# Attention and FFN in one kernel: 78 steps of the hand-kept plan are given to the engines at another tick

## The chip, the cores and the metric

One core of a Trainium2 chip runs the whole program in one launch. The metric is device time in microseconds of that core. The kernel before takes 844.36 us, the median of 3 runs (844.21 to 844.95).

## The reference

Attention over 8 sequences of 576 positions with 8 heads of 64; heads 0 to 3 see a window of the last 32 positions, heads 4 to 7 every fourth of the last 128. Its output, seen as 4608 tokens of 512 numbers, goes through a feed-forward layer of width 2048 with an exact GELU.

```python
scores = scale * np.matmul(q, k.transpose(0, 1, 3, 2))
scores = np.where(masks[None, :, :, :], scores, -1000000000.0)
attn = np.exp(scores - np.max(scores, axis=-1, keepdims=True))
attn = attn / (np.sum(attn, axis=-1, keepdims=True) + 1e-09)
x = np.matmul(attn, v)          # 8 x 8 x 576 x 64, then to 4608 x 512
h = x @ w_in                    # 4608 x 2048
g = 0.5 * h * (1.0 + erf(h / sqrt(2)))
out = g @ w_out                 # 4608 x 512
```

## The kernel before, in words

The tokens are cut into nine chunks of 512: the first 512 positions of each sequence (chunks 0 to 7), and the eight remainders of 64 together (chunk 8). Attention works on a pair of heads at a time ("5.2" is chunk 5, head pair 2): scores on TensorE (L307), softmax in place on ScalarE (`softmax`, L428, one activation with a running sum per 64 keys), the division and a transpose on VectorE (`norm_half`, `turn_both`), four exchanges of rows by DMA (`swap_keys`, L383), the weighted sum on TensorE (`av_four`, L573; `av_last`, L530, for chunk 8) and the way back to SBUF (`x_back` on VectorE, L586; `x_wide` on ScalarE, L594).

Every number of the feed-forward layer is held as a high part and a residual ("low") in fp32r, and a product of two blocks is three matmuls for each of two halves of 128 rows: high by high, residual by high, high by residual.

Chunks 0 to 2 go through the feed-forward layer plainly (L605, L628). From chunk 3 on the kernel takes two chunks and two blocks of the weights as a 2 by 2 block product and forms it from seven products, M1 to M7, in place of eight (L1044). There are three pairs of chunks, (3, 4), (5, 6) and (8, 7), and four groups of weights. One pair with one group is called a **round** here: 14 products for the first layer (the **H half**: M1 to M7 for two output blocks, called e0 and e1), then 14 for the second (the **O half**: M1, M5, M6, M2, M7, M3, M4, each for e0 and e1). A product is six matmuls of 128 x 512. R1 to R12 are the rounds in order of time; R1 begins 326.0 us after the span's start.

In a H half ScalarE copies M1 from its bank to another one (L1069) before M6 may be added in the first, stashes M6 and M5 (L1065), and applies GELU; VectorE adds (L1073, L1076). The results are the four block values B11, B12, B21, B22 and the combinations T1 = B12 - B11 (L1092), T3 = B22 - B12 (L1093), T2 = B22 - T1 (L1094), T4 = B21 - T2 (L1095). Of seven of these ScalarE rounds the high part (L1090) and VectorE subtracts the residual (L1091): the operands of the O half, B11 for M1, T1 for M5, T2 for M6, B21 for M2, T3 for M7, B22 for M3, T4 for M4.

In an O half sums of products are formed in PSUM: ScalarE copies M1 out of banks 2 and 3 (L1101, "first copy"), M6 is added there, ScalarE copies the sum again to banks 0 and 1 (L1101, "second copy") as soon as these are emptied of M5, then M7 is added, then M4. Four accumulators in SBUF, C11, C12, C21 and C22, and M5 take the banks over: by ScalarE in the first round of a pair (L1107), by VectorE in the others (L1109). C22 must be taken out of banks 2 and 3 before M4 may start there, C21 before the next round's M1 is copied into them.

The operands of the next pair of chunks (`combine`: high part L923, residual L928, combinations L936) are made the same way, beside the last round of the pair before. The weights of the seven products come from DRAM into a ring of five tiles (`ring_load`, L997), one tile for the two products that share it, on SyncE's queue, which also carries the loads of q, k and v, the exchanges, and the finished outputs (L1129).

The order of the work is written by hand. The products stand in a fixed order. All other work from chunk 2's attention on is a list of 1237 **steps**; `add(at, rank, gen)` gives a step a tick (one product is one tick; R1 begins at tick 96 and each round is 28 ticks) and a rank. The list is sorted by tick, rank and place in the list (L1183), and after each product the steps whose tick has come are given to the engines (`upto`, L758). Each engine takes its instructions strictly in that order, so a tick sets only which instruction stands ahead of which on an engine; it sets no time.

Of the kernel before, what the change touches and what calls it, by code (L numbers as in the profile page):

```python
# [46 lines left out]
TICKS = 28  # L47
ORDER = (2, 3, 0, 1)
SLOTS = 5

SUBTRACT = ()
SCHEDULE = """
# [35 lines left out]
def attn_ffn(ctx: ExitStack, tc: tile.TileContext, qk, qk_lp, qk_ld, v, v_ld, w, outT):  # L88
# [662 lines left out]
    steps = []  # L751

    def add(at, rank, gen):
        steps.append((at, rank, len(steps), gen))

    at = 0

# [57 lines left out]
    def prepare(u, at, dt):  # L815
        s = {}
        add(at, 5, unit_whole(s, u))
        for i in range(4):
            add(at + (3 + .5 * i) * dt, 5, unit_sums(s, u, i))
        for n in range(2):  # L820
            add(at + (4 + n) * dt, 6, unit_high(s, u, n))
            add(at + (4.5 + n) * dt, 6, unit_low(s, u, n))
            add(at + (6 + n) * dt, 6, keep_sums(s, u, n))
# [135 lines left out]
    def ring_tile(n):  # L959
        n %= SLOTS  # L960
        if n not in ring:
            ring[n] = xg.tile([P, 2, N], F32R, tag="xg", name="ring")
        return ring[n].rearrange("p a (b c) -> p (a b) c", b=2)
# [23 lines left out]
    def ring_load(n):  # L987
        yield "q"
        j, q, kind, m = tiles[n]
        to = ring_tile(n).bitcast(F32)  # L990
        off = DM if kind == "O" else 0
        if m in SUMS:
            src, off = sd[ORDER[q]][:, SUMS[m]], off // 2
        else:
            i, k = HELD[kind][m]
            src, off = wd[ORDER[q]][i], off + 2 * P * k
        nc.sync.dma_start(to, src.rearrange("p u (l c) -> p (u l) c", l=2)[:, :, off:off + 2 * P])  # L997
    for n in range(len(tiles)):
        add(P0 - 7.5 + .3 * n if n < SLOTS else P0 + last_use[n - SLOTS] + 2, 4, ring_load(n))

# [332 lines left out]
```

## Time and profile before

| | |
|---|---|
| median of 3 runs | 844.36 us |
| the profiled execution | 845.09 us, span 843.3 us |
| TensorE matmul busy | 816.3 us, 97% of the span |
| TensorE weight load busy | 661.5 us, 78% |
| VectorE, ScalarE busy | 562.7 us (67%), 503.7 us (60%) |
| mean granted TensorE clock | 0.996 of full speed |
| DMA | 212.31 MB, 252 GB/s |

A timeline row gives the start, the length and the instructions run together, and in brackets how long the engine sat idle ahead of them and which instruction ended that wait. A wait for "issue" is one for which the profile names no releaser. A matmul row's length ends with the last matmul's result; the next row's start tells when TensorE's array was free again, so lengths of stretches are taken from start to start.

### The profile page before, as it was taken

How to read it: one execution, taken by the hardware profiler on the slowest of the kernel's cores; microseconds unless marked ns; L12 is line 12 of the kernel's file. 1: busy time of each engine (PE TensorE's matmuls, PEld its weight loads, DVE VectorE, ACT ScalarE, POOL GpSimd, SP SyncE). 2: the span in 40 equal slices, each digit the busy share in tenths (PEclk: the TensorE clock that was granted, in tenths of full speed). 3: DMA queues.
4: the chain of work that ended last, by engine and by line, in shares of the span. 5: the costliest groups of instructions: out<-in, count | busy, mean ns of one | idle time of the engine just before them, and what ended most of it. 6: DMA issues, size and time to landing. Idle time of an engine off the chain costs nothing.

```text
span 843.3 us, 19925 instructions
## 1 busy us (share of the span) xinstructions
PE 816.3 (97%) x8396; PEld 661.5 (78%) x8396; DVE 562.7 (67%) x675; ACT 503.7 (60%) x1149; POOL 57.7 (7%) x80
## 2 busy tenths in 40 slices
PE   7899999999999999989999999999999999999997
PEld 5687888888888888868787777777787788888885
DVE  8888863347676797545757786734657886172847
ACT  7597833735747565676555674857766646453442
POOL 2000020222305220000000000000000000000000
PEclk9999999999999999999999999999999999999999
DMA  9997478945998869876767688856466677665664
GB/s 362 416 419 303 152 300 323 373 154 189 318 359 296 294 212 331 254 233 194 271 203 274 193 296 258 284 185 225 144 218 222 205 249 238 197 189 191 197 197 152
DMA packets 118296, 212.31 MB, mean 252 GB/s; under 512 B 6848, under 2 KB 92864, under 8 KB 110784
## 3 DMA queue, kind: packets, MB, share of 16 engines
q1 hardware_dynamic: 118064, 210.79, 72.2%
q8 instruction: 66, 1.08, 0.5%
q10 hardware_dynamic: 144, 0.26, 0.1%
q14 instruction: 22, 0.18, 0.1%
HBM read 161.21 MB, written 42.99 MB: 242 GB/s over the span
## 4 chain that ended last, share of the span: by engine, by line
PE 75%; ACT 11%; DVE 10%; issue 2%; DMA 1%; SPq 0%; DVEq 0%; ACTq 0%
PE ps L1044 37%; PE ps L628 16%; PE ps L605 16%; PE ps L307 3%; ACT g L1090 3%; ACT sm L428 2%; PE ps L573 2%; DVE g L1091 2%; ACT ps L1101 1%; ACT xn L594 1%; DVE g_value L1093 1%; DMA raw_qk<-qk 1%; ACT L428 1%; DVE acc L1094 1%; DVE g_value L1076 1%
## 5 line engine op out<-in xcount | busy, mean ns | idle before, releaser
L1044 PE MATMUL ps<-g,ring 128*128 128x512 f32 x1008 | 239.0, 394 | 10.5 <-issue 3.4
L1044 PE MATMUL ps<-xc,ring 128*128 128x512 f32 x1008 | 237.1, 393 | 2.7 <-ACT ps L1069 2.7
L1044 PEld LDWEIGHTS ps<-g,ring 128*128 128x128 f32 x1008 | 188.3, 189 | 58.3 <-DVE g L1091 6.1
L1044 PEld LDWEIGHTS ps<-xc,ring 128*128 128x128 f32 x1008 | 189.0, 189 | 43.5 <-ACT ps L1069 3.3
L1091 DVE TENSOR_TENSOR g<-g_value,g 128x1024 fp32r<-128x1024 f32 x73 | 89.1, 1222 | 106.9 <-ACT g L1090 106.9
L605 PE MATMUL ps<-x,weight 128*128 128x512 f32 x576 | 137.5, 392 | 0.9 <-DVE x L550 0.6
L628 PE MATMUL ps<-g,weight 128*128 128x512 f32 x576 | 135.6, 392 | 0.0
L605 PEld LDWEIGHTS ps<-x,weight 128*128 128x128 f32 x576 | 107.1, 188 | 24.4 <-DVE x L550 1.0
L628 PEld LDWEIGHTS ps<-g,weight 128*128 128x128 f32 x576 | 107.3, 188 | 22.7
L1090 ACT CAST g<-g_value 128x1024 fp32r<-128x1024 f32 x73 | 76.2, 1048 | 38.2 <-DVE g_value L1093 21.9
L428 ACT ACTIVATE sm<-sm,st 128x64 f32<-128x64 f32 (+1 forms) x224 | 75.6, 339 | 0.9 <-DVE st L359 0.7
L617 DVE TENSOR_TENSOR g<-gf,g 128x512 fp32r<-128x512 f32 x48 | 35.9, 748 | 55.4 <-ACT g L107 55.3
L612 ACT ACTIVATE gf<-ps 128x512 f32<-128x512 f32 x48 | 28.7, 598 | 67.7 <-PE ps L605 67.4
L789 POOL TENSOR_TENSOR whole<-weight 128x512 f32<-128x512 f32 x32 | 45.9, 1466 | 132.3 <-PE ps L628 69.2
L1109 DVE TENSOR_TENSOR acc<-ps,acc 128x1024 f32<-128x1024 f32 (+1 forms) x48 | 49.1, 1037 | 5.3 <-PE ps L1044 5.1
L1065 ACT COPY u<-ps 128x512 f32<-128x512 f32 x48 | 28.2, 586 | 32.5 <-PE ps L1044 29.6
L1069 ACT COPY ps<-ps 128x512 f32<-128x512 f32 x24 | 13.7, 570 | 55.6 <-PE ps L1044 30.5
L428 ACT ACTIVATION_READ_ACCUMULATOR sm<-sm,st 128x1 f32 x224 | 42.2, 188 | 0.0
L307 PEld LDWEIGHTS ps<-raw_qk 64*32 64x32 f32 x2304 | 26.5, 110 | 11.3 <-issue 8.4
L307 PE MATMUL ps<-raw_qk 64*32 64x64 f32 (+1 forms) x2304 | 31.5, 236 | 3.5 <-issue 2.1
L1074 ACT ACTIVATE g_value<-g_value 128x512 f32<-128x512 f32 x24 | 15.2, 633 | 31.0 <-DVE g_value L1073 31.0
L928 DVE TENSOR_TENSOR xc<-xn,xc 128x1024 fp32r<-128x1024 f32 x21 | 25.5, 1217 | 10.4 <-ACT xc L923 10.3
(131 smaller groups left out, 797.6 us busy)
## 6 DMA issues: line engine op xcount, KB each, us to landing
ring<-sd SPq DMA_DIRECT2D x96, 512.0 KB, 3.8
ring<-wd SPq DMA_DIRECT2D x72, 512.0 KB, 4.6
v_sb<-v SPq DMA_DIRECT2D x17, 1024.0 KB, 7.0
raw_qk<-qk SPq DMA_DIRECT2D x32, 512.0 KB, 7.9
wd<-weight SPq DMA_DIRECT2D x16, 1024.0 KB, 12.2
sd<-sums SPq DMA_DIRECT2D x16, 1024.0 KB, 6.9
raw_w<-w SPq DMA_DIRECT2D x15, 1024.0 KB, 18.9
weight<-wd SPq DMA_DIRECT2D x8, 1024.0 KB, 9.2
```

The source lines that it names most:

```text
L307: nc.tensor.matmul(s.sc[32 * r:32 * r + 32, h, c0:c0 + s.nk], x[:, q0:q0 + 32], x[:, k0:k0 + s.nk], start=s.c > 1, stop=s.c > 1 or u == NU ...
L428: nc.scalar.activation(t, s.sc[:, h, at:at + 2 * KB] if s.c < 2 else t, AF.Exp, bias=st[:, 0], scale=SCALE if s.c < 2 else -1.0, accum_out ...
L605: nc.tensor.matmul(bank, weights[f][:, t, cc * P:(cc + 1) * P], x[:, xx], start=n == 1 and i == 0, stop=n == parts and i == 2)
L612: nc.scalar.activation(gf, bank, AF.Gelu)
L617: nc.vector.tensor_sub(g[:, 1], gf, g[:, 0])
L628: nc.tensor.matmul(ps[:, d], weights[f][:, t, DM + d * P:DM + (d + 1) * P], gs[f][:, u], start=f == first and n == 0, stop=f == last and n ...
L789: nc.gpsimd.tensor_add(to, x, y)
L1044: nc.tensor.matmul(ps[:, bank], lhs, rhs, start=start and i == 0, stop=i == 5, skip_group_check=True)
L1065: nc.scalar.copy(spare_tile[k, i], bank("a", i))
L1090: add(base + t, 4, run("a", lambda k=k, v=v: nc.scalar.copy(operand(k, 0, final), val(v))))
L1091: add(base + t1, 4, run("d", lambda k=k, v=v: sub(operand(k, 1, final), val(v), operand(k, 0, final))))
L1109: plus(to, src, to)
```

## The change

`add` looks up the step's place in the list in a new table, `SHIFTED`, and adds the number found there to the tick. 78 of the 1237 steps have an entry, from -6 to +8.5 ticks; no step is added, dropped or altered. Lines below the table stand ten further down than before. Two of the table's seven lines:

```diff
@@ -47,6 +47,16 @@
 ORDER = (2, 3, 0, 1)
 SLOTS = 5
+
+SHIFTED = {
+    268: 8.5, 275: 1, 287: -0.7, 290: 2.5, 293: 0.9, 299: -1.6, 302: 0.6, 303: 0.6, 311: -6, 313: 3.1, 316: 2.5, 332: -3.1,
...
+    1196: -0.1, 1199: -0.9, 1200: -1.4, 1208: 1, 1211: 0.3, 1224: 0.3,
+}
...
     def add(at, rank, gen):
-        steps.append((at, rank, len(steps), gen))
+        steps.append((at + SHIFTED.get(len(steps), 0), rank, len(steps), gen))
```

Of the moved steps 14 are pairs of softmax activations and 10 other steps of attention, 17 are residuals or high parts of operands, 7 are combinations T1 to T4 of a round, 14 are copies and drains of PSUM banks, 6 are ring loads, 6 belong to `combine`, 3 to GELU and its sums, and one is a store.

VectorE, O half of R1. Before: residuals of T1 and T2 (`g<-g_value`, `g<-acc`), residual of B21, then T3 (L1093), residual of T3, then T4 (L1095).

```order
L1076 TENSOR_TENSOR g_value<-ps,u 128x512
L1091 TENSOR_TENSOR g<-g_value,g 128x2x512
L1091 TENSOR_TENSOR g<-acc,g 128x2x512
L1091 TENSOR_TENSOR g<-g_value,g 128x2x512
L1093 TENSOR_TENSOR g_value<-g_value 128x1024
L1091 TENSOR_TENSOR g<-g_value,g 128x2x512
L1095 TENSOR_TENSOR g_value<-g_value,acc 128x1024
```

Now:

```order
L1086 TENSOR_TENSOR g_value<-ps,u 128x512
L1101 TENSOR_TENSOR g<-g_value,g 128x2x512
L1101 TENSOR_TENSOR g<-acc,g 128x2x512
L1103 TENSOR_TENSOR g_value<-g_value 128x1024
L1101 TENSOR_TENSOR g<-g_value,g 128x2x512 x2
L1105 TENSOR_TENSOR g_value<-g_value,acc 128x1024
```

T3 stands ahead of the residual of B21, where it stood behind it. The same is done in R2, R5 and R8.

VectorE, end of R4's O half, from the drain of C11 on. Before: drains of C11 and C22 (`acc<-ps`, 1024 wide), a combination of the next pair (L936), the drain of C12, the four instructions of `norm_half` and `turn_both`, another L936, and the two drains of C21 (512 wide).

```order
L1109 TENSOR_TENSOR acc<-ps,acc 128x1024
L1091 TENSOR_TENSOR g<-g_value,g 128x2x512
L1109 TENSOR_TENSOR acc<-ps,acc 128x1024
L936 TENSOR_TENSOR xn<-xn 128x1024
L1109 TENSOR_TENSOR acc<-ps,acc 128x1024
L364 TENSOR_SCALAR st<-st 128x16
L366 RECIPROCAL st<-st 128x16
L368 TENSOR_TENSOR sm<-sm,st 128x1024
L375 STREAM_TRANSPOSE turned<-sm 128x1024
L936 TENSOR_TENSOR xn<-xn 128x1024
L1109 TENSOR_TENSOR acc<-ps,acc 128x512 x2
```

Now, from the drain of C22 on:

```order
L1119 TENSOR_TENSOR acc<-ps,acc 128x1024
L1101 TENSOR_TENSOR g<-g_value,g 128x2x512
L374 TENSOR_SCALAR st<-st 128x16
L376 RECIPROCAL st<-st 128x16
L378 TENSOR_TENSOR sm<-sm,st 128x1024
L1119 TENSOR_TENSOR acc<-ps,acc 128x1024
L385 STREAM_TRANSPOSE turned<-sm 128x1024
L1119 TENSOR_TENSOR acc<-ps,acc 128x512
L946 TENSOR_TENSOR xn<-xn 128x1024
L1119 TENSOR_TENSOR acc<-ps,acc 128x512
L1119 TENSOR_TENSOR acc<-ps,acc 128x1024
```

The drain of C11 went from the head of the list to its end, one L936 far ahead of it, and the other L936 between the two drains of C21.

TensorE, end of R4 and H half of R5 (`ps<-raw_qk` is the scores of 8.2, `ps<-v_sb,turned` is `av_four` of 8.0). Before:

```order
L1044 MATMUL ps<-g,ring 128x512 x84
L1044 MATMUL ps<-xc,ring 128x512 x24
L307 MATMUL ps<-raw_qk 32x96 x32
L1044 MATMUL ps<-xc,ring 128x512 x30
L573 MATMUL ps<-v_sb,turned 32x64 x64
```

Now:

```order
L1054 MATMUL ps<-g,ring 128x512 x84
L1054 MATMUL ps<-xc,ring 128x512 x18
L317 MATMUL ps<-raw_qk 32x96 x32
L1054 MATMUL ps<-xc,ring 128x512 x36
L583 MATMUL ps<-v_sb,turned 32x64 x64
```

The scores of 8.2 stand one product earlier, between M6 e0 and M6 e1. It is the only place where TensorE's order differs.

## Rows read from the trace of the kernel before

**Rows 1.** Waits of TensorE from 326 us on: total us, times, longest
```profile
PE ps L1044 <- issue: 3.4, 4, 0.9
PE ps L1044 <- ACT ps L1069: 2.7, 2, 1.8
PE ps L1044 <- ACT ps L1101: 2.7, 5, 1.3
PE ps L1044 <- DVE g L1091: 2.3, 2, 1.5
PE ps L1044 <- ACT acc L1107: 2.0, 2, 1.1
PE ps L530 <- ACT xn L594: 1.1, 1, 1.1
```
**Rows 2.** Timeline of TensorE: two halves of R9, the last half (R12)
```profile
685.70 19.20 PE L1044 MATMUL ps<-xc,ring 128*128 128x512 f32 x84
704.74 19.20 PE L1044 MATMUL ps<-g,ring 128*128 128x512 f32 x84
...
818.98 19.98 PE L1044 MATMUL ps<-g,ring 128*128 128x512 f32 x84
```
**Rows 3.** Windows over seven O halves (R1 to R5, R7, R8): R4, and their sum
```profile
480.71:503.74 23.03, 20.21 (x86) 15.46 (x85) 19.20 (x21) 17.67 (x48) 0.00 (x0) 1.00 0.81 291
...
sum 149.40, PE 138.95 PEld 109.00 DVE 120.33 ACT 110.43 POOL 0.00; mean PE 19.85 PEld 15.57 DVE 17.19 ACT 15.78 POOL 0.00
```
**Rows 4.** Timeline of TensorE: R5's H half, R6's O half
```profile
508.41 4.61 PE L1044 MATMUL ps<-xc,ring 128*128 128x512 f32 x12 [1.79 <-ACT ps L1069]
512.94 1.00 PE L307 MATMUL ps<-raw_qk 64*32 64x96 f32 x64
...
582.72 1.60 PE L530 MATMUL ps<-turned,v_wide 32*64 32x32 f32 x96 [1.10 <-ACT xn L594]
584.25 7.32 PE L1044 MATMUL ps<-g,ring 128*128 128x512 f32 x24
591.50 1.60 PE L530 MATMUL ps<-turned,v_wide 32*64 32x32 f32 x96
```
**Rows 5.** Windows of the two slow stretches; third number from the right: granted clock
```profile
508.40:513.00 4.60, 4.59 (x20) 3.38 (x25) 1.03 (x1) 2.10 (x3) 0.00 (x0) 0.63 0.83 273
584.25:591.50 7.25, 7.25 (x30) 5.59 (x25) 4.66 (x5) 5.48 (x18) 0.00 (x0) 0.76 0.96 363
```
**Rows 6.** Timeline of VectorE in R1's O half
```profile
355.10 1.22 DVE L1091 TENSOR_TENSOR g<-g_value,g 128x1024 fp32r<-128x1024 f32 x1 [2.81 <-ACT g L1090]
356.24 1.22 DVE L1093 TENSOR_TENSOR g_value<-g_value 128x1024 f32<-128x1024 f32 x1
```
**Rows 7.** Timeline of ScalarE in R1's O half
```profile
357.49 1.05 ACT L1090 CAST g<-g_value 128x1024 fp32r<-128x1024 f32 x1 [1.76 <-DVE g_value L1093]
358.45 1.00 ACT L1107 COPY acc<-ps 128x1024 f32<-128x1024 f32 x1
...
360.02 0.58 ACT L1101 COPY ps<-ps 128x512 f32<-128x512 f32 x1
```
**Rows 8.** Timeline of TensorE in R1's O half: M7 and M4
```profile
360.65 5.99 PE L1044 MATMUL ps<-g,ring 128*128 128x512 f32 x24 [1.26 <-ACT ps L1101]
367.57 3.04 PE L1044 MATMUL ps<-g,ring 128*128 128x512 f32 x12 [0.93 <-ACT acc L1107]
```
**Rows 9.** Timeline of VectorE where R4 meets R5
```profile
505.91 1.18 DVE L936 TENSOR_TENSOR xn<-xn 128x1024 f32<-128x1024 f32 x1
507.02 1.28 DVE L1109 TENSOR_TENSOR acc<-ps,acc 128x512 f32<-128x512 f32 x2
```
**Rows 10.** Timeline of SyncE's queue in R5's H half
```profile
510.25 3.25 SPq L383 DMA_DIRECT2D turned<-turned  x4
513.60 0.54 SPq L997 DMA_DIRECT2D ring<-sd  x1
```
**Rows 11.** Ring loads between 500 and 530 us
```profile
DMA to landing us min/median/max: 5.4/5.5/5.8
```

5 rows, old and new, of the table SHIFTED are left out of this document.

## The prediction

> **What bounds the kernel now.** I read the waits of TensorE first, then its timeline, then windows over single halves, and last the timelines of the two engines that release it. TensorE is the bound: from R9 on it does not wait at all, and the rows there show what an undisturbed half costs. One half starts 19.04 us after the other, though its own row is 19.20 long [rows 2]: TensorE's array is free 0.16 us before the last result is out. So 14 products cost 19.04 us (0.2267 a matmul), and each wait that a row shows has cost its idle time and 0.16 more.
>
> Rounds R1 to R8 are not undisturbed. The list of waits from R1 on adds up to 14.2 us [rows 1]. The windows show more: seven O halves without attention matmuls take 149.40 us together [rows 3], where seven undisturbed ones take 133.28, so they lose 16.1 us, R4's most (23.03 - 19.04 = 3.99). Of this, 10.4 us are 13 of the listed waits (those for L1101, L1107, L1091 and "issue") and 2.1 their restarts; 3.6 are waits too short for a row. Most of it stands at two places of every half: the first product M7, which waits for the second copy of the banks (L1101), and the first M4, which waits until C22 is drained (L1107; where VectorE drains, the four waits put down to "issue" stand at M4 too) [rows 1, 8].
>
> Three more losses lie outside these halves. In R5's H half M6 waits 1.79 us for L1069; then 12 matmuls last from 508.41 to 512.94 [rows 4], 4.53 us where 2.72 is due, at a mean granted clock of 0.63 [rows 5], so part of that stretch ran at the lower of the two levels. In R6's O half the weighted sum of 8.2 waits 1.10 us for `x_wide`, and the next 24 matmuls take 7.25 us in place of 5.44 [rows 4], at 0.76 [rows 5]. In R7's H half M6 waits for L1069 again, 0.9 us, the other part of that 2.7 [rows 1]. R12's O half is 0.78 us longer than R9's [rows 2].
>
> **The change, place by place.** No instruction is added or dropped, so what changes is which wait is last. What can be won, in the profile's own time:
>
> - seven O halves: 16.1;
> - R5's H half: 1.79 + 0.16 + 1.81 of slow clock = 3.8;
> - R6's O half: 1.10 + 0.16 + 1.81 = 3.1;
> - R7's H half: 0.9 + 0.16 = 1.1;
> - R12: 0.5 of the 0.78.
>
> That is 24.6 us. Whether it is won I decide by walking the new orders with the old durations.
>
> *R1's O half.* VectorE sits idle 2.81 us up to 355.10, waiting for the high part of B21, and only then computes T3 at 356.24 [rows 6]; ScalarE sits idle 1.76 us up to 357.49, waiting for T3 [rows 7]. With T3 ahead, VectorE starts it at 355.10 - 2.81 = 352.3 and has it at 353.5. ScalarE was free for T3's high part at 357.49 - 1.76 = 355.7, and a pair of softmax activations that stood in front of it (about 0.6 us: the drain at 358.45, one such pair and then the copy at 360.02 [rows 7]) is moved behind; it starts at 355.1, 2.4 us earlier. The drain of M5 and the second copy follow it, so the copy starts at 357.6 and ends at 358.2; M7 wanted it at 360.65 - 1.26 = 359.4 [rows 8]. The first wait goes with 1.2 us to spare. The drain of C22, on ScalarE in this round, moves by the same 2.4 and by 0.6 for a second pair moved behind it: 3.0 us, where M4's start moves by the 1.26 + 0.16 won before and needs 0.93 more [rows 8], together 2.4. The second wait goes with about 0.6 to spare. The softmax pairs put behind are read only by `norm_half`, which stands behind the drains too: ScalarE's idle time covers them.
>
> *R2, R3, R5, R7.* The same pattern: T3 goes forward in R2 and R5, the first copies of M1 are put together ahead of the exponentials (R2, R3), exponentials move behind T3's high part or the second copy (R2, R3, R7). On VectorE the drain of C22 follows the residuals directly. In each I find the second copy and the drain early by 0.4 us or more.
>
> *R4 and R8.* Here M5 waits for the residual of T1, 1.5 us in R4 and 0.8 in R8 [rows 1], since VectorE still works for the next pair's operands. One such residual (a step of 1.14 us, 355.10 to 356.24 [rows 6]) is moved behind, and in R4 half of an `x_back` forward into idle time. In R4 the two are more than the 1.5 + 0.16 needed; in R8 the residual meets 0.8 + 0.16. But B21's residual in R4 now stands behind a residual of the next pair and M5's drain and comes within 0.1 us of M2's need: I keep 0.3 us.
>
> *Where R4 meets R5.* M6 waits for L1069, L1069 for the drains of C21, and these start at 507.02 behind an L936 [rows 9], 3.3 us after R5's begin. Now both L936 and the drain of C11, about 1.1 us each, stand elsewhere; the first drain of C21 starts some 1.0 us after R5's begin, and the scores of 8.2, put one product earlier, give the second copy another 0.9 us. The stall goes, and I expect the slow clock after it to go as well: both slow stretches follow a stall, and 133 us of dense matmuls from R9 on show none.
>
> *SyncE's queue there.* It is the new tight place. A store of C21 is moved ahead of six exchanges and two ring loads, and a ring load waits behind the store of C11, whose drain comes last. Four exchanges take 3.25 us to issue, and the next ring load goes out at 513.60 [rows 10] and lands 5.5 us later [rows 11]. I walk the queue to 510 for that load, landing at 515.6, against 516.2 for its first product, M3; the exchanges land between 512 and 514.3, against 513.5 for `av_four`. Cost: at best 0, at worst a stall of 1 to 1.8 us followed by a slow stretch as in [rows 4], 3.6. I take 1.5.
>
> *R6.* `x_wide` of 8.3 no longer waits behind T2's high part and a GELU: it ends 2.6 us earlier, against the 1.10 + 0.16 needed. *R7's seam* follows, since the drains of C21 come earlier with R6's exponentials.
>
> The two loads of q and k that are issued earlier wait for nothing later than what is done by then. The other ring loads move by half a tick.
>
> Kept back: 0.3 for R4, 1.5 for SyncE's queue, and 1.8, half of the 3.6 us of waits too short for a row, which no walk resolves. 24.6 - 3.6 = 21.0 us. From the profiled 845.09 that is 824.1; that execution is 0.73 above the median of 844.36, so the forecast is **823.4**. All won gives 819.8.
>
> On the repeated gap: the rows say that M7's bank copy is late because ScalarE waits for T3, not because a bank is missing [rows 7, 8]. The Trainium skill ("Perfetto Trace Analysis", section Optimization Strategy) says that the same gap repeating on the engine that should be saturated can mean too little SBUF or PSUM for the next tile; by that, a new order would leave those gaps where they are, and the time would be the 833.4 of the third rival below.
>
> **Rivals.**
>
> *A. The queue in R5 is late.* For it: the margins above are under 1 us, and exchanges and stores there each wait for VectorE. Against it: it is the only seam at which exchanges, stores and ring loads meet. 823.4 + 3.6 = 827.0.
>
> *B. The second wait of each half stays.* M4's waits for C22 (3.4 for "issue" and 2.0 for L1107, six places [rows 1]) stay while M7's go, if M7 starting earlier only makes M4 ask earlier. For it: the margins there are the smaller ones. Against it: the drains were moved by more than the first wait in R1. 5.4 + 6 x 0.16 = 6.4 us less won: 829.8.
>
> *C. The banks bind.* All bank waits stay (2.7 + 2.0 + 3.4 = 8.1 in 11 places, with restarts 9.9, hence 10.0 less won): 833.4. Against it: the idle rows of both engines [rows 6, 7].
>
> *D. Slower: the seam between rounds becomes the wait.* The moved work (exponentials, C11's drain, an L936 between C21's two drains) ends up at the seam, and M6 waits for L1069 there in seven seams as it did in R5: 1.79 + 1.81 = 3.6 us each [rows 4], 25.2 in all, against 21.0 won: 848.6. It decides where the first drain of C21 ends later than about 2.1 us after the round's begin (two products, 2.72, less a copy of 0.58 [rows 7]), or 3.5 where score matmuls stand ahead of M6. Against it: I walk that end to 0.6 to 2.1 us after the begin, the latest in R7, where scores stand ahead.
>
> *E. No change:* the waits are replaced by equal ones; 844.4.
>
> **How the numbers follow.** Forecast 0.57, A 0.13, B 0.14, C 0.06, D 0.05, E 0.05. The range 819 to 832 holds the forecast with all won, A and B with 2 us of slack, 0.84 together; C, D and E are left out. A measurement of this kernel can tell about 0.2%, 1.7 us, from no change. Faster by more than that: 0.57 + 0.13 + 0.14 + 0.06 = 0.90; within it 0.05; slower 0.05.
>
> **What would show it.** Right: in the new profile R1's wait for L1101 is gone and ScalarE no longer sits idle for T3; O halves of R1 to R8 are 19.0 to 19.6 us long; no row of 12 or 24 matmuls lasts 1.8 us too long; granted clock near 1.00 from 508 on. SyncE's queue: a wait of L1054 or L583 for a DMA in R5 shows A. B shows as waits of M4 for drains, C as waits for the second copy with ScalarE free before it, D as M6 waiting for L1079 at the rounds' begins. A saving under 11 us makes the walk wrong.

## The result and the profile after

The changed kernel takes 822.83 us, the median of 4 runs (822.32 to 823.60), beside 844.29 for the kernel before (4 runs, 842.83 to 844.95). The ratio is 0.9749, with a 95% interval of 0.9732 to 0.9766. Its profiled execution took 823.21 us, with a span of 821.4.

The page of the changed kernel, its busy times and its chain of waits:

```profile
PE 807.6 (98%) x8396; PEld 660.2 (80%) x8396; DVE 561.9 (68%) x675; ACT 502.9 (61%) x1149; POOL 57.7 (7%) x80
...
PE 90%; DMA 4%; DVE 3%; ACT 1%; issue 1%; SPq 1%; DVEq 0%
```

Every engine still does the same work. TensorE is busy 807.6 us where it was 816.3, since the short waits inside rows and the slower clock of [rows 5] counted as busy; the other 13 us of the gain were idle time. VectorE and ScalarE are as busy as they were.

Waits of TensorE from 320 us on: the six lines of [rows 1], 14.2 us together, have become one.

```profile
PE ps L1054 <- DMA ring<-wd: 1.2, 2, 0.6
```

The timeline of TensorE in the changed kernel shows where these two stand, and the O halves of R1, R2, R3, R4, R5 and R12 (84 matmuls each):

```profile
347.91 19.21 PE L1054 MATMUL ps<-g,ring 128*128 128x512 f32 x84
...
389.47 19.20 PE L1054 MATMUL ps<-g,ring 128*128 128x512 f32 x84
...
430.99 19.20 PE L1054 MATMUL ps<-g,ring 128*128 128x512 f32 x84
450.81 3.00 PE L1054 MATMUL ps<-xc,ring 128*128 128x512 f32 x12 [0.63 <-DMA ring<-wd]
...
473.65 19.34 PE L1054 MATMUL ps<-g,ring 128*128 128x512 f32 x84
493.60 4.37 PE L1054 MATMUL ps<-xc,ring 128*128 128x512 f32 x18 [0.62 <-DMA ring<-wd]
...
516.85 19.38 PE L1054 MATMUL ps<-g,ring 128*128 128x512 f32 x84
...
797.52 19.58 PE L1054 MATMUL ps<-g,ring 128*128 128x512 f32 x84
```

R1's half was cut into three rows by the waits of [rows 8]; now it is one row of 19.21, as R9's was [rows 2]. What is left are two waits of 0.6 us at the first product of R4 and of R5, whose tile of the weights has not landed.

Lengths of the halves from start to start, in microseconds. An O half is counted up to the next round's first matmul, so R3's and R4's hold the two waits for the ring:

| half | before | after | won |
|---|---|---|---|
| O of R1, R2, R3 | 22.10, 21.31, 21.12 | 19.04, 19.04, 19.82 | 6.63 |
| O of R4 | 23.03 | 19.95 | 3.08 |
| O of R5, R7, R8 | 21.41, 20.19, 20.24 | 19.21, 19.19, 19.04 | 4.40 |
| H of R5 | 26.69 | 23.25 | 3.44 |
| O of R6 | 25.31 | 22.55 | 2.76 |
| H of R7 | 23.21 | 22.22 | 0.99 |
| the other H halves of R1 to R8 | 135.08 | 135.37 | -0.29 |

That is 21.01 us from R1 to R8. R12's row is 0.40 shorter, R1 begins 0.44 earlier, and 21.85 of the 21.88 us between the two profiled executions (845.09 and 823.21) are found. R1's begin is no gain of the change: in the thirteen traces of this case it lies between 325.57 and 327.75 us, and two of the kernel before have 326.01 and 327.75.

R1's O half is where the prediction's walk can be held against the trace step by step. VectorE of the changed kernel:

```profile
351.76 1.22 DVE L1103 TENSOR_TENSOR g_value<-g_value 128x1024 f32<-128x1024 f32 x1
354.66 2.36 DVE L1101 TENSOR_TENSOR g<-g_value,g 128x1024 fp32r<-128x1024 f32 x2 [1.68 <-ACT g L1100]
```

ScalarE at the same place:

```profile
353.58 1.99 ACT L1100 CAST g<-g_value 128x1024 fp32r<-128x1024 f32 x2
355.48 1.00 ACT L1117 COPY acc<-ps 128x1024 f32<-128x1024 f32 x1
...
357.06 0.57 ACT L1111 COPY ps<-ps 128x512 f32<-128x512 f32 x1
```

T3 now fills VectorE's idle time of [rows 6]; VectorE still waits for B21's high part, 1.68 us, but with nothing urgent behind it. ScalarE's wait for T3 [rows 7] is gone: B21's and T3's high parts run together (353.58), the drain of M5 follows, and the second copy runs from 357.06 to 357.63, some 1.2 us before M7 begins (at 358.8, 48 undisturbed matmuls after 347.91).

### The profile page after: what moved, and what is told of

The parts are those of the page before. It is cut to its first block, busy times and chain, and to the rows that moved or that the text cites. A ratio compares the mean times of both kernels' runs of the same rounds, so it can differ in the third digit from the quotient of the medians.

```text
span 821.4 us, 19919 instructions
## 1 busy us (share of the span) xinstructions
PE 807.6 (98%) x8396; PEld 660.2 (80%) x8396; DVE 561.9 (68%) x675; ACT 502.9 (61%) x1149; POOL 57.7 (7%) x80
## 4 chain that ended last, share of the span: by engine, by line
PE 90%; DMA 4%; DVE 3%; ACT 1%; issue 1%; SPq 1%; DVEq 0%
PE ps L1054 50%; PE ps L638 16%; PE ps L615 16%; PE ps L317 3%; DMA ring<-wd 3%; PE ps L583 2%; DMA raw_qk<-qk 1%; PE ps L540 1%; DVE g L1101 1%; PE ps L529 1%; PE ps L480 0%; ACT sm L438 0%; ACT g L1100 0%; PE ps L739 0%; SPq L266 0%
## 5 line engine op out<-in xcount | busy, mean ns | idle before, releaser
L1054 PE MATMUL ps<-g,ring 128*128 128x512 f32 x1008 | 231.8, 390 | 0.0
L1079 ACT COPY ps<-ps 128x512 f32<-128x512 f32 x24 | 13.7, 571 | 52.5 <-PE ps L1054 45.1
L367 DVE SCALAR_TENSOR_TENSOR sm<-ps,masks 128x1024 f32<-128x1024 f32 x13 | 15.9, 1222 | 23.5 <-PE ps L317 23.5
```

Source lines behind the costliest of these rows:

```text
L1054: nc.tensor.matmul(ps[:, bank], lhs, rhs, start=start and i == 0, stop=i == 5, skip_group_check=True)
```

## The experiments

All kernels below give the engines the same operations as the two kernels, but for one that says so. "The change" is the changed kernel; each ratio is to the kernel before, with its 95% interval. The change itself took 822.83 and 823.81 us in two sets of runs, so a difference of 1 us between whole runs of different sets says little; where time went is read from the lengths of halves, each from one trace.

| run | time (us) | ratio |
|---|---|---|
| the four steps of T3 alone | 839.59 | 0.9943 (0.9927 to 0.9959) |
| the change without them | 827.34 | 0.9801 (0.9786 to 0.9816) |
| the two steps of x_wide alone | 843.30 | 0.9993 (0.9983 to 1.0002) |
| the change without them | 825.32 | 0.9782 (0.9765 to 0.9800) |
| the change without 15 steps around R4's end | 829.56 | 0.9839 (0.9802 to 0.9876) |
| the change without 14 softmax steps | 827.37 | 0.9808 (0.9792 to 0.9825) |
| the change with a stall put into R10 | 824.70 | 0.9772 (0.9757 to 0.9787) |
| the change, two v loads later | 821.81 | 0.9744 (0.9729 to 0.9758) |
| the same once more | 821.65 | 0.9736 (0.9723 to 0.9750) |
| the change once more, beside it | 823.81 | 0.9761 (0.9747 to 0.9774) |

**T3 alone.** The kernel before with four entries of the table, the steps that make T3 in R1, R2, R5 and R8.

```diff
+SHIFTED = {688: -1.2, 734: -0.6, 878: -3, 1016: -0.6}
```

> The kernel before with the four entries alone that put T3 ahead of B21's residual (R1, R2, R5, R8). Walked with the durations of before: in R1 ScalarE gets T3 1.76 us earlier, so M7's wait of 1.26 goes and a part of M4's 0.93; in R2 both waits go (0.21 and 0.86); in R5 both go but T2's residual comes 0.6 us too late for M6; R8 unchanged. Theory 'the order of VectorE was the first cause': about 4 us won, 840. Rival 'T3 alone moves the wait to the next in line': 0 to 1.5 us won. Rival 'T3 is most of it': over 10 us won, 834 or less.

Measured: 839.59 us, 4.6 below the 844.21 of the kernel before beside it. The O halves of R1, R2 and R5 are 1.84, 1.64 and 1.67 us shorter, R8's 0.05. TensorE in R1's O half of this kernel:

```profile
349.28 16.53 PE L1054 MATMUL ps<-g,ring 128*128 128x512 f32 x72
366.64 3.06 PE L1054 MATMUL ps<-g,ring 128*128 128x512 f32 x12 [0.83 <-ACT acc L1117]
```

Here M7's wait of [rows 8] is gone, and M4's has stayed almost as it was, 0.83 for 0.93. In R2 and R5 both waits are gone, but in R5 M6 now waits 0.23 us for T2's residual, as expected. In R3 and R4, where T3 was not moved, M7 (0.36 and 0.54) and M4 (0.85 and 0.84) wait as before. The first theory holds: the order of VectorE was the first cause where T3 was moved, and other places need other steps.

**The change without T3's steps.**

```diff
-    688: -1.2, 734: -0.6, 878: -3, 1016: -0.6,
```

> The change without the four entries that put T3 ahead. Theory: in R1 M7 waits again, about 1.3 us, in R5 about 1.0, in R2 and R8 the other entries have left enough slack (over 1 us) and nothing comes back: 2.6 us slower than the change, 825.4. Rival 'each place needs all its entries': what T3 alone won, 4 us or more, comes back. Rival 'the softmax entries do the work': 0.

Measured: 827.34 us, 4.5 above the change. R1's O half is 2.43 us longer, R5's 1.45, R8's 0.64; R2's does not change (19.07). TensorE in R1's and R5's O half:

```profile
360.81 5.98 PE L1054 MATMUL ps<-g,ring 128*128 128x512 f32 x24 [1.27 <-ACT ps L1111]
367.06 3.01 PE L1054 MATMUL ps<-g,ring 128*128 128x512 f32 x12 [0.27 <-ACT acc L1117]
...
530.86 8.70 PE L1054 MATMUL ps<-g,ring 128*128 128x512 f32 x36 [1.05 <-ACT ps L1111]
```

The first row is the wait of [rows 8] back at its size, 1.27 for 1.26. M7's two waits came as expected, but the 2.6 us did not hold: R1 lost more than that wait, and R8 was to lose nothing; the rival's 4 us is nearer. The whole is as large from either side, 4.6 and 4.5, but its parts are not: in R2 other moved steps do what T3's does, and in R8 T3 counts only with the others.

**The seam between R4 and R5.** The change without the entries that clear R4's O half and the head of R5: the drain and the store moved there, the two L936, the scores of 8.2, the `x_back` half, the residuals, and single steps beside them, one pair of exponentials among them.

```diff
-    332: -3.1, 344: 0.3, 347: -1.1, 358: -1, 454: 0.1, 460: 4.6, 461: -4, 466: 1.9, 467: -0.3,
-    814: -0.3, 818: 1.6, 824: 1.6, 829: 0.3, 834: 6.6, 840: -2.5,
```

> The change without its 15 entries between the H half of R4 and the H half of R5 (T2's and T1's residuals, the L936, C11's drain, the store of C21, the scores of 8.2 and what stands beside them). Theory 'these entries win R4's O half and R5's H half and nothing else': R4's O half is back near 23.0 us and R5's H half near 25.2 (its length in two runs with the stall but without a slow stretch), all other halves as in the change: 5 to 6 us slower than the change, 828.4. Rival 'later halves lean on it': more than 7 us. Rival 'the rest of the change has made them unneeded': under 2 us.

Measured: 829.56 us (826.95 to 833.70). In the profiled execution (827.51) only R4's O half (23.04) and R5's H half (25.11) come back, 4.95 us together, and the two waits for the ring are gone. TensorE there:

```profile
477.74 8.04 PE L1054 MATMUL ps<-g,ring 128*128 128x512 f32 x34 [1.46 <-DVE g L1101]
486.29 6.03 PE L1054 MATMUL ps<-g,ring 128*128 128x512 f32 x24 [0.50 <-ACT ps L1111]
493.16 2.98 PE L1054 MATMUL ps<-g,ring 128*128 128x512 f32 x12 [0.85 <-issue]
...
500.65 3.02 PE L1054 MATMUL ps<-xc,ring 128*128 128x512 f32 x12 [1.79 <-ACT ps L1079]
```

All four waits of this place are back at their old sizes, M6's at the 1.79 of [rows 4]. But the 12 matmuls behind it take 3.02 us, not the 4.6 of [rows 4]: the wait came back without the slow clock. Two of the four runs took 831.61 and 833.70 us, far more than these halves explain, at mean granted clocks of 0.997 and 0.995; they have no trace.

**The softmax steps.** The change without the 14 entries that put pairs of exponentials at other places.

```diff
-    268: 8.5, 275: 1, 290: 2.5, 293: 0.9, 299: -1.6, 313: 3.1, 316: 2.5, 344: 0.3,
-    362: -1.2, 372: 1.6, 389: 3.4, 390: 7, 398: -3.1, 412: 2.5,
```

> The change without its 14 softmax entries. Theory, by the walk: M4 waits about 1.2 us in R1's O half, M7 0.9 in R3's, M4 about 0.4 in R5's, M6 0.6 in R6's, and M6 at R7's begin about 1.9, since the last pair of 7.1 then stands behind the copies of chunk 8; R2 and R7's O half have slack: 5.2 us slower than the change, 828. Rival 'softmax only fills idle time on ScalarE': under 1 us.

Measured: 827.37 us, 4.5 above the change. The O halves of R1, R2, R5, R6 and R7 are 1.2, 0.5, 0.4, 1.0 and 0.5 us longer, R7's H half 0.3 where the walk said 1.9. R3's O half is 20.59, 1.55 above the undisturbed 19.04: M7 waits 0.35 and 0.47 us there, where the walk said 0.9. TensorE in R1, in R3 and at the head of R7:

```profile
365.79 3.06 PE L1054 MATMUL ps<-g,ring 128*128 128x512 f32 x12 [0.82 <-ACT acc L1117]
...
445.05 1.65 PE L1054 MATMUL ps<-g,ring 128*128 128x512 f32 x6 [0.35 <-ACT ps L1111]
447.18 7.23 PE L1054 MATMUL ps<-g,ring 128*128 128x512 f32 x30 [0.47 <-ACT ps L1111]
...
590.79 16.61 PE L1054 MATMUL ps<-xc,ring 128*128 128x512 f32 x72 [0.16 <-ACT ps L1079]
```

In R1 this is M4's wait, the one that T3 alone left: T3 and the exponentials are the two halves of what R1 won. The walk's terms hold in R1, R3 and R5; R6's is 1.0 for 0.6, R7's begin is far off, and R2 and R7's O half, which were to have slack, lose 0.5 each. The total, 4.5 for 5.2, is nearer than its parts.

**x_wide.** The kernel before with the two entries that bring `x_wide` of 8.3 forward in R6: one moves it, the other puts a GELU behind it.

```diff
+SHIFTED = {382: -0.6, 899: 0.6}
```

> The kernel before with two entries alone: the two that put both copies of chunk 8's attention output (x_wide of 8.2 and 8.3) next to each other in R6. If the three losses there are simply undone, 1.10 + 0.16 + 1.81 us of slow clock, it is 3.1 us faster, 841.2. By the walk the wait of the weighted sum goes, but ScalarE reaches R7's begin only about 1.2 us earlier while TensorE comes 2.6 earlier, so M6's wait there grows from 0.9 to about 2.3 us and may bring a slow stretch of its own: 0 to 1.2 us won, 843 to 844.

Measured: 843.30 us over 10 runs, not to be told from the kernel before. The wait of L530 in [rows 4] is gone, and R6's O half is 24.31 us long, 1.0 less. Two smaller waits stand in it instead:

```profile
583.25 4.80 PE L1054 MATMUL ps<-g,ring 128*128 128x512 f32 x18 [0.27 <-ACT ps L1111]
...
595.74 3.00 PE L1054 MATMUL ps<-g,ring 128*128 128x512 f32 x12 [0.49 <-issue]
```

Granted clock of this half, third number from the right:

```profile
574.27:598.58 24.31, 23.42 (x278) 18.36 (x276) 15.22 (x14) 22.32 (x54) 0.00 (x0) 1.00 0.70 239
```

So R6's O half, even without the stall and at full clock throughout, is 1.76 us longer than in the changed kernel: copies of banks and drains were late there too, and other steps of the change bring them forward. At R7's begin M6 waits 1.02 us for L1079, not the 2.3 of the walk: TensorE comes 1.0 us earlier, not 2.6. The total was expected rightly, by a route that did not happen.

**The change without x_wide's steps** asks the other way round.

```diff
-    382: -0.6, 899: 0.6,
```

> The changed kernel without its two entries for x_wide in R6. Theory: x_wide of 8.3 ends late again and the weighted sum in R6's O half waits for it, by up to 1.1 us; if that stall is what brings the slow stretch there, the next 24 matmuls take 7.25 us in place of 5.44 and the half 25.5 (22.55 now), in all 825.8. Rival: the stall alone brings no slow stretch, as in R10: the half is 23.8 and the time 824.1. Second rival: R6's other moved steps have freed ScalarE anyway and x_wide is in time: 822.8.

Measured: 825.32 us (824.19 to 827.77), 1.5 above the change run beside it. TensorE in R6's O half:

```profile
566.77 1.60 PE L540 MATMUL ps<-turned,v_wide 32*64 32x32 f32 x96 [1.12 <-ACT xn L604]
568.30 5.73 PE L1054 MATMUL ps<-g,ring 128*128 128x512 f32 x24
```

The window behind it:

```profile
570.00:575.00 5.00, 5.00 (x90) 4.04 (x88) 3.80 (x5) 4.99 (x16) 0.00 (x0) 1.00 1.00 385
```

The wait is back at 1.12, the half is 23.74 us, 1.19 longer, and the next 24 matmuls are not slow (5.73 for 7.32 in [rows 4]) though the DMA engines are as busy. In the profiled execution, then, the first rival holds. The other executions do not all fit it: 824.19 us came at a mean granted clock of 0.999, 826.26 at 0.998 and 827.77 at 0.996, so in the longer ones the clock fell somewhere, and no trace shows where. That the stall brings a slow stretch in some of them is not excluded.

**A stall by itself.** The change with seven copies of `masks`, a small table, onto itself put on ScalarE ahead of the M1 copy in R10, where nothing else waits. They are added work; nothing is left out.

```diff
+    for _ in range(7):
+        add(348.5, 0, run("a", lambda: nc.scalar.copy(masks, masks)))
     steps.sort(key=lambda t: t[:3])
```

> The change, with seven extra copies of a small table that is no longer used, on ScalarE, ahead of the copy L1079 that M6 of R10 waits for: a stall of about 1.8 us in a stretch of dense 128 x 512 products, with no attention matmul within 60 us. Theory 'a stall of this size brings the slow stretch': the round is longer by the stall, 0.16 and another 1.8 us, at a mean granted clock below 0.8 over the next 5 us; about 3.8 us slower than the change, 826.6. Rival 'the slow stretch needs the small matmuls or the load of the DMA engines that stood around it in R5 and R6': stall and 0.16 only, clock 1.00, 824.8.

Measured: 824.70 us, 1.9 above the change. TensorE in R10's H half:

```profile
706.81 16.62 PE L1054 MATMUL ps<-xc,ring 128*128 128x512 f32 x72 [1.75 <-ACT ps L1079]
```

Granted clock during the stall and behind it:

```profile
702.00:707.00 5.00, 3.25 (x15) 2.40 (x14) 0.00 (x0) 4.43 (x10) 0.00 (x0) 1.00 0.53 165
707.00:712.00 5.00, 5.00 (x23) 4.11 (x23) 0.00 (x0) 2.01 (x4) 0.00 (x0) 1.00 0.36 114
```

The half is 21.09 us, 2.05 longer: the idle time, the restart and little else. In this execution a stall as long as [rows 4]'s did not bring the lower clock. DMA is much less busy here than at [rows 5], so this run alone says nothing of a stall where DMA is busy; the trace without x_wide's steps shows one there, in R6, with no slow stretch behind it.

**The kernel before, once more**, with nothing edited, to see whether both slow stretches of [rows 5] are its own.

> The kernel before, unchanged, profiled a second time, to see whether the slow stretches of R5 and R6 are there again. Theory 'a slow stretch comes by chance, in some executions': with the same waits (1.79 and 1.10) at least one of the two stretches is at a clock of 1.00, R5's H half 25.2 us in place of 26.69 or R6's O half 23.5 in place of 25.31, and the next waits are longer by part of it. Rival 'these stalls always bring it': both again.

One execution: 845.39 us. TensorE at R5's M6:

```profile
510.22 3.01 PE L1044 MATMUL ps<-xc,ring 128*128 128x512 f32 x12 [1.81 <-ACT ps L1069]
```

Granted clock there, and behind R6's wait:

```profile
510.22:514.00 3.78, 3.78 (x76) 2.95 (x76) 1.02 (x1) 2.81 (x5) 0.00 (x0) 1.00 0.93 307
...
584.50:591.80 7.30, 7.30 (x36) 5.62 (x28) 4.70 (x5) 5.54 (x18) 0.00 (x0) 0.77 0.95 364
```

R5's slow stretch is not there, with the same wait ahead of it; R5's H half is 25.18 us instead of 26.69. R6's is there, as in [rows 5]. Among five traces with the wait of 1.8 us at R5 (the two of the kernel before, T3 alone, x_wide alone, the seam undone), one has the slow stretch. Among four with the wait of 1.1 us at R6 (the two of the kernel before, T3 alone, the change without x_wide's steps), two have it: both of the kernel before, neither of the others.

What R6's slow stretch cost shows beside T3 alone, which has the same wait there. First a row of the kernel before, from R6's H half, for 24 matmuls ahead of a weighted sum at full clock; then R6's O half with T3 alone:

```profile
565.97 5.73 PE L1044 MATMUL ps<-xc,ring 128*128 128x512 f32 x24
...
576.91 1.60 PE L540 MATMUL ps<-turned,v_wide 32*64 32x32 f32 x96 [1.09 <-ACT xn L604]
578.44 6.44 PE L1054 MATMUL ps<-g,ring 128*128 128x512 f32 x24
...
592.55 3.00 PE L1054 MATMUL ps<-g,ring 128*128 128x512 f32 x12 [0.48 <-issue]
```

Its granted clock behind the wait:

```profile
578.44:584.80 6.36, 6.25 (x30) 4.27 (x24) 3.77 (x4) 4.59 (x15) 0.00 (x0) 1.00 1.02 398
```

The clock is full, yet the 24 matmuls take 0.71 us longer than the first row, which no row resolves, and M4 waits 0.48 later on. With the slow clock they took 1.59 longer (7.32). Behind the slow matmuls of [rows 4] there is no such wait. The half is 25.18 us long here, and 25.31 with the slow stretch.

**The two waits that are left.** SyncE's queue in the changed kernel where R4 ends:

```profile
479.85 0.61 SPq L272 DMA_DIRECT2D v_sb<-v  x1
480.52 0.90 SPq L266 DMA_DIRECT2D raw_qk<-qk_ld  x2
482.00 0.52 SPq L1007 DMA_DIRECT2D ring<-wd  x1
```

Ring loads issued between 480 and 495 us:

```profile
DMA to landing us min/median/max: 7.8/9.1/10.1
```

A load of v of 1 MB and two of q and k of 1 MB each are issued just ahead of a ring load, and the four ring loads from there on take 7.8 to 10.1 us to land, where [rows 11] had 5.5. The same burst stands in the kernel before; there TensorE lost 4 us in R4's O half and asked later. The edit issues the loads of v for 6.2 and 8.0 three ring loads later:

```diff
+    330: 5.9, 353: 5.9,
```

> The change with two more entries: the loads of v for 6.2 (in R3) and 8.0 (in R4), 1 MB each, are issued 5.9 ticks later, behind the ring load of the next round's M1. Theory 'the two new waits for the ring come from the burst of v, q and k that goes out just ahead of that ring load': both waits go (0.63 and 0.62 with their 0.16 in the profile of the change; 0.18 and none in that of the run with the added stall, which has the same orders there): 0.5 to 1.5 us faster than the change, 821.8. Rival 'the DMA engines are full there whatever the order': no difference, or the wait moves to another tile.

Measured: 821.81 us, and the trace shows no wait of TensorE from R1 on. (The 0.18 us that the expectation counts among the ring's waits is one for VectorE's L378 in that trace.) Since that is only 1.0 us below the change, with overlapping intervals, both kernels were run once more, beside each other.

> The two v loads 5.9 ticks later, once more. If the two waits for the ring are what it wins, no wait from R1 on and 1.0 us less than the changed kernel beside it; if the 1.0 us seen was scatter between calls, the two are within 0.5 us of each other.

> The changed kernel once more, beside the one with the two spread loads, so that the two share their runs of before. Waits of TensorE for the ring at the head of R4's and R5's first product, 0.6 us each; 822.8 (0.975 of before).

Measured: 821.65 us (821.50 to 822.18) and 823.81 us (823.50 to 824.15). The longest run of the one is below the shortest of the other. In the change the wait stands at R5 alone this time, and is longer:

```profile
493.91 4.37 PE L1054 MATMUL ps<-xc,ring 128*128 128x512 f32 x18 [1.09 <-DMA ring<-wd]
```

The queue of the edited kernel at the same place:

```profile
478.92 1.09 SPq L266 DMA_DIRECT2D raw_qk<-qk_ld  x2
481.07 0.52 SPq L1007 DMA_DIRECT2D ring<-wd  x1
483.96 0.38 SPq L1007 DMA_DIRECT2D ring<-sd  x1
486.69 0.52 SPq L1007 DMA_DIRECT2D ring<-wd  x1
487.26 0.61 SPq L272 DMA_DIRECT2D v_sb<-v  x1
```

And its ring loads between 480 and 495 us:

```profile
DMA to landing us min/median/max: 5.7/6.4/7.2
```

With the 1 MB of v three ring loads later, the median ring load here lands in 6.4 us instead of 9.1, and the tile is there in time, though the DMA engines are busy throughout in both. R1 to R8 take 336.94 us instead of 338.40, of which the one wait with its restart is 1.25; R1 also begins 0.57 us earlier, which nothing in the edit explains, so the edit wins less than the 2.2 us between the medians. Nor do the two waits come every time: four traces have the change's orders up to there, and R4 and R5 wait 0.63 and 0.62, nothing and 1.09, 0.65 and nothing, and (with the added stall) not for the ring at all, at median landings of 9.1, 9.5, 8.3 and 7.7 us. Both traces with the later loads have none, at 6.0 and 6.4. This version is faster than both kernels.

## Why the prediction was right, and where it was off

**The bound and the sum.** Forecast 823.4, measured 822.83. The prediction summed what could be won to 24.6 us and kept 3.6 back; the same terms (the halves of the table but its last row, and R12's 0.40) gave 21.70. *Seven O halves, 16.1*: 14.11 won, the rest mostly the two waits for the ring, 1.25 idle and two restarts, and 0.45 in R4, R5 and R7. *R5's H half, 3.8*: 3.44. *R6's O half, 3.1*: 2.76. *R7, 1.1*: 0.99. *R12, 0.5*: 0.40. No wait that the walk said would go has stayed in any of the eight rounds. The entries taken out in the experiments are 34 of the 78; the other 44 were not tried by themselves, and what they win is read from the halves alone.

**R1's walk.** R1 begins 0.44 us earlier in the changed kernel. With this added, T3 starts at 352.2 (predicted 352.3), the second copy at 357.5 (357.6). That T3 takes M7's wait away and the exponentials put behind take M4's is shown from both sides: of the 3.06 us won in R1's O half, T3 alone wins 1.84; without T3 2.43 are lost, without the softmax steps 1.22, with 0.82 of it M4's wait.

**R4 and the seam.** Undoing the seam's steps brought back just these two halves in the profiled execution, so they and no others carry that gain. Of the 0.3 us kept for B21's residual in R4 about 0.14 were lost: its O half is one row of 19.34, with no wait in it.

**The slow clock is the step that was off.** The prediction said "I expect the slow clock after it to go as well: both slow stretches follow a stall", and put 1.81 us for it into each of two terms. The sizes about fitted the profiled execution, from which the sum was made, but the reason did not hold. They are also somewhat large: 2.72 and 5.44 us are not what 12 and 24 matmuls take where attention matmuls follow, but 2.94 and 5.66 (510.22 to 513.16 in the second trace, 565.97 to 571.63 in the first), so a slow stretch cost 1.59 and not 1.81. In R5 the same kernel with the same wait ran at full clock the next time and was 1.51 us shorter in that half; of the 3.44 won there, about 1.9 come from the change (25.18 to 23.25). In R6 the slow stretch cost next to nothing: with the wait but at full clock (T3 alone) the half was 25.18 us, with both (before) 25.31. Copies and drains that were late behind the slow matmuls cost nearly as much where these were not slow. R6's gain is thus about 1.0 to 1.2 for `x_wide` and the rest from banks and drains that come earlier, the exponentials' part 1.0; that the prediction had the amount without its parts is luck.

The whole runs say the same. Of thirteen runs of the kernel before, taken beside T3 alone, six had a mean granted clock of 1.000, which leaves no room for a stretch like those of [rows 5] (one costs about 0.002, an estimate: 1.59 of 843 us). They took 843.35 to 844.78 us, median 844.2; the four at 0.998 took 843.31 to 844.04, the three at 0.996 844.68 to 845.79. So runs without a slow stretch were not 3.2 us shorter, and the change wins its 21 us against them too. What they lost in its place no trace shows.

**SyncE's queue.** 1.5 us were kept for it in R5's H half, for M3's tile and the weighted sum. There nothing waits. The ring waits stand ahead of that, at M1 of R4 and R5, 0.63 and 0.62 idle and 0.16 each for the restart: 1.6 us. That the 1.5 met these 1.6 is luck: I walked the queue where the change reorders it and did not ask what the faster TensorE asks of it ahead of that. The 1.8 kept for short waits were hardly needed: the O halves of R1, R2 and R8 are at the undisturbed 19.04, those of R5 and R7 0.15 above it.

**The rivals.** *A* (queue late in R5, 827.0) fell: its mechanism showed at another place, at 1.6 us and no slow stretch. *B* (M4's waits stay, 829.8) fell; R1 with T3 alone shows what it would look like. *C* (the banks bind, 833.4) fell with no bank wait left. The Trainium skill ("Perfetto Trace Analysis", section Optimization Strategy) reads a gap that repeats on the engine meant to be saturated as a possible lack of SBUF or PSUM; here the trace does not agree, since the 11 gaps that *C* counts went with no bank or tile added. *D* (the seam becomes the wait, 848.6) fell: no M6 waits for L1079. *E* fell with them.

## What to carry to other kernels

A repeated gap on a busy engine is worth tracing back two releases: here copy, high part, T3, and an instruction in front of T3 that had to wait while T3 did not. When such gaps close, look next at what the faster engine asks for earlier, a place ahead of the edit as well as behind it, and at the loads of other tiles that stand in the same queue. A slow-clock stretch seen in one execution is not yet a price of the code in front of it, and where the engine would have waited behind it anyway its length is no price at all; take a second profile of the unchanged kernel before putting it into a sum.

## What the hardware showed that was not expected

- The same wait of 1.8 us at R5 was followed by a lowered clock in one trace of five, the wait of 1.1 us at R6 in two of four, and a wait of 1.75 us in R10, in its one trace, by none. What decides is open. Both slow stretches of R6 are the kernel before's, so there it may be the code around it and not chance; how busy DMA was does not tell them apart (a share of 0.95 and 0.96 in the slow stretches, 1.00 and 1.02 without one).
- Some kernels with such a wait also spread more from run to run. With the seam undone, four runs took 826.95, 827.51, 831.61 and 833.70 us at mean granted clocks of 0.999, 0.999, 0.997 and 0.995; the version without any wait stayed within 821.50 and 822.18. Where in the longer runs the clock fell was not recorded.
- A slow stretch on an engine that would have waited anyway costs little: R6's O half took 25.31 us with it and 25.18 without it (T3 alone), where its rows suggest 1.6.
